# Moving the last sum of w2 behind the key-value masks, and the zero rows of the FFN block from GpSimd to VectorE

## The chip, the cores and the metric

The kernel runs on one core of one Trainium2 chip. The metric is the device time of one execution in microseconds, lower is better; medians of several executions are quoted. Each execution also has a *span*, the time from its first to its last recorded instruction. The device time is longer than the span, by something between 1.2 and 1.7 us in this case; I call the difference the *time outside the span*, and it will matter.

In lines of a profile PE is TensorE's matrix products and PEld its weight loads, DVE is VectorE, ACT ScalarE, POOL GpSimd and SP SyncE; L819 is line 819 of the kernel, and `<-` in brackets names what ended the idle time before.

## The reference, cut to what matters

```python
xn = layernorm(x)                                  # x: 2048 x 640, bf16
q, k, v = split(xn @ wqkv)                         # 32 heads of 20
pq, pk = phi(q), phi(k)
kv  = einsum("bhsd,bhse->bhde", pk, v)             # linear attention
s   = (pq @ kv) / (pq @ sum(pk)) @ wo
g   = silu(relu(xn @ w1) @ w2)                     # w1: 640 x 1728, w2: 1728 x 640
out = x + s * g
```

1728 is thirteen and a half blocks of 128, so the last block of the FFN's hidden rows is half used and its other rows must be zero. Those are the "zero rows".

## The kernel before: the parts concerned

The kernel computes the FFN product with a scheme of seven block products in place of eight. For that it needs four sums and differences of blocks of w2, made once by VectorE (`u_T(1)` to `u_T(4)`), and sums of blocks of the hidden layer (`u_S`). Close to the same place it forms the key-value matrix of all heads in one product, keeps the blocks on the diagonal by multiplying with a mask (`kv_group`), and multiplies them with wo (`W_block`).

```python
def kv_group(cs, b):                      # called for ps bank 5, then for ps bank 7
    ...                                   # 15 matmuls on PE into ps[b]
    tt(o_..., ps[b][...], mv6[...], ALU.mult, ...)      # the mask, on VectorE

def W_block(c, b):                        # banks b, b+1
    sc.group("PE", [... wo ...], R=[("wo", c), ("kv", c)], W=[("ps", b), ("ps", b + 1)])
    ...                                   # copy out (VectorE for c in 1, 4, else ScalarE)
    ...                                   # small DMAs on SP put the rows together

    u_T(2)
    divide(0)
    ...
    u_T(4)                                # the last sum of w2: 128 x 2240
    ...
    for n, fn in enumerate(us):           # us: the seven products of the first pair
        fn()
        if p == 0:
            if n == 0:
                kvs()                     # both kv_groups
            if n == 1:
                W_block(0, 4)
                W_block(1, 6)
```

A small scheduler gives every instruction its waits from what it reads and writes. Each engine works its list in order, so the place of `u_T(4)` in the text is its place in VectorE's queue. The constants, the zero rows among them, are made by GpSimd some way into the FFN's first layer:

```python
def build_consts():
    sc.op("POOL", lambda eng: eng.memset(hT[:, NF, :], 0.0), W=[("hz",)])   # 128 x 2048, bf16
    sc.op("POOL", lambda eng: eng.memset(sel[:, :], 1.0 / 32), W=[("sel",)])
    ...
```

Of the kernel before, what the change touches and what calls it, by code (L numbers as in the profile page):

```python
# [208 lines left out]
def bass_recurrent_scan__linear_attn_block__dense_activation_relu__prompt_kernel(  # L209
# [18 lines left out]
    NF = FF // P  # L228
# [36 lines left out]
    hT = regH[:, :].rearrange("p (f s) -> p f s", f=NK)  # L265
# [87 lines left out]
    sc = Sched(nc, NDS)  # L353
# [38 lines left out]
    def wk_load(k0, k1):  # L392
# [2 lines left out]
            W=[("wk", k) for k in range(k0, k1)])  # L395

    sc.op("DVE", lambda eng: eng.memset(zero[:, :], 0.0), W=[("zero",)])
    sc.op("ACT", lambda eng: eng.activation(out=msum[:, 3, 0:1], in_=zero[:, 0:1], func=ACTF.Copy),
          R=[("zero",)], W=[("msum", 3, 0)])
    sc.allow_unread.add(("msum", 3, 0))  # L400
# [29 lines left out]
    fill(32)  # L430

    def build_consts():
        sc.op("POOL", lambda eng: eng.memset(hT[:, NF, :], 0.0), W=[("hz",)])
        sc.op("POOL", lambda eng: eng.memset(sel[:, :], 1.0 / 32), W=[("sel",)])
        for u, base, mul in ((0, P // 2 - 1, -1), (1, -P // 2, 1)):
            sc.op("POOL", lambda eng, u=u, base=base, mul=mul: eng.affine_select(
                out=sel[:, u:u + 1], in_=sel[:, u:u + 1], compare_op=ALU.is_ge, fill=0.0, base=base, pattern=[[0, 1]],
                channel_multiplier=mul), R=[("sel",)], W=[("sel",)])
        sc.op("POOL", lambda eng: eng.memset(mh[:, :, :], 1.0), W=[("mh",)])
        sc.op("POOL", lambda eng: eng.affine_select(out=mh[:, :, :], in_=mh[:, :, :], compare_op=ALU.is_ge, fill=0.0,  # L440
                                                    base=0, pattern=[[P, C], [-DH, H]], channel_multiplier=1),
              R=[("mh",)], W=[("mh",)])
        sc.op("POOL", lambda eng: eng.affine_select(out=mh[:, :, :], in_=mh[:, :, :], compare_op=ALU.is_ge, fill=0.0,
                                                    base=DH - 1, pattern=[[-P, C], [DH, H]], channel_multiplier=-1),
              R=[("mh",)], W=[("mh",)])
        for lo, n, off in ((0, 6, 0), (6, 2, P - 2 * DH)):
            mt = mv6[:, lo:lo + n]
            key = ("mv6", lo)
            sc.op("POOL", lambda eng, mt=mt: eng.memset(mt, SC), W=[key])
            sc.op("POOL", lambda eng, mt=mt, n=n, off=off: eng.affine_select(  # L450
                out=mt, in_=mt, compare_op=ALU.is_ge, fill=0.0, base=-off, pattern=[[-DH, n]], channel_multiplier=1),
                R=[key], W=[key])
            sc.op("POOL", lambda eng, mt=mt, n=n, off=off: eng.affine_select(
                out=mt, in_=mt, compare_op=ALU.is_ge, fill=0.0, base=off + DH - 1, pattern=[[DH, n]], channel_multiplier=-1),
                R=[key], W=[key])
# [283 lines left out]
    def hz(keys):  # L739
        return sc._hazards([], keys)  # L740
# [62 lines left out]
    def load_recip(i):  # L803
        r = RS[i]
        keys = [("xnT", t) for t in range(12, T)] if r == 0 else [("zhi",), ("zlo",)] + ekeys + \
            [("gS", 1, q) for q in (1, 2, 4)]
        dma("SP", lambda eng: eng.dma_start(Rr[r], scr[:, schunk(i)].rearrange("(m p) s -> p m s", p=P)),
            R=[("scr", i)], W=[("Rr", r)], extra=hz(keys))
# [9 lines left out]
    def tt(out, in0, in1, op, R, W, extra=()):  # L818
        sc.op("DVE", lambda eng: eng.tensor_tensor(out=out, in0=in0, in1=in1, op=op), R=R, W=W, extra=extra)  # L819
# [322 lines left out]
    for c in range(VC):  # L1142
        r0 = VR * c if c < VC - 1 else D - P
        dma("SP", lambda eng, c=c, r0=r0: eng.dma_start(wo_sb[:, c, :], A_wo[r0:r0 + P, :]),
            W=[("wo", c)], extra=[last_norm[0]])
# [99 lines left out]
    def kv_group(cs, b):  # L1245
        fns = []
        for i, c in enumerate(cs):
            n0, n1 = VR * c, min(VR * c + VR, D)
            r0 = VR * c if c < VC - 1 else D - P
            for k in range(C):  # L1250
                fns.append(lambda eng, k=k, i=i, n0=n0, n1=n1, r0=r0: eng.matmul(
                    ps[b][:, VR * i:VR * i + n1 - n0], lhsT=wv_sb[:, k, r0:r0 + P], rhs=GT[:, k, n0:n1],
                    start=(k == 0), stop=(k == C - 1), skip_group_check=True))
        sc.group("PE", fns, R=[("wv",)] + gtk, W=[("ps", b)])
        for part in ([c for c in cs if c < VC - 1], [c for c in cs if c == VC - 1]):
            if not part:
                continue
            c0, nc_ = part[0], len(part)
            n0 = VR * c0
            nh = (min(n0 + VR, D) - n0) // DH  # L1260
            m0 = 0 if c0 < VC - 1 else 6
            st = D + VR
            q0 = VR * (c0 - cs[0])
            o_ = reg3[:, st * c0:st * (c0 + nc_)].rearrange("p (c x) -> p c x", x=st)[:, :, 0:nh * DH]
            tt(o_.rearrange("p c (h e) -> p c h e", e=DH),
               ps[b][:, q0:q0 + nc_ * nh * DH].rearrange("p (c h e) -> p c h e", c=nc_, e=DH),
               mv6[:, m0:m0 + nh].unsqueeze(1).unsqueeze(3).to_broadcast([P, nc_, nh, DH]), ALU.mult,
               [("ps", b), ("mv6", m0)], [("kv", c) for c in part], [lastG])
# [50 lines left out]
    def u_T(i):  # L1319
        b11, b12 = w2_sb[:, 0:KH, 0:HN], w2_sb[:, 0:KH, HN:D]  # L1320
        b21, b22 = w2_sb[:, KH:NK, 0:HN], w2_sb[:, KH:NK, HN:D]
        if i == 3:
            tt(uT[3], b22, b12, ALU.subtract, w2keys, [("uT", 3)], hz([("gT", 2)]))
        elif i == 2:
            tt(uT[2], uT[3], b11, ALU.add, w2keys + [("uT", 3)], [("uT", 2)], hz([("gT", 3)]))
        elif i == 4:
            tt(uT[4], b21, uT[2], ALU.subtract, w2keys + [("uT", 2)], [("uT", 4)], hz([("gT", 4)]))
        else:
            tt(uT[1], b12, b11, ALU.subtract, w2keys, [("uT", 1)], hz([("gT", 1)]))
# [174 lines left out]
    def flush():  # L1504
        while late:
            late.pop(0)()
# [40 lines left out]
    divide(0)  # L1547
    load_recip(1)
    load_recip(2)
    u_T(4)  # L1550

    def load_xre():
        for jx in range(4):
            dma("SP", lambda eng, jx=jx: eng.dma_start(
                xre[:, 4 * jx:4 * jx + 4, :], x2[512 * jx:512 * (jx + 1), :].rearrange("(t p) n -> p t n", p=P)),
                W=[("xre", jx)], extra=[lastG])

    def kvs():
        kv_group([0, 1, 2], 5)
        kv_group([3, 4, 5], 7)  # L1560


    for p in range(8):
        us = U_steps(p)
        os_ = O_steps(p - 1) if p else None
        at = 1
        for n, fn in enumerate(us):
            fn()
            if p == 0:
                if n == 0:  # L1570
                    kvs()
                if n == 1:
                    W_block(0, 4)
                    W_block(1, 6)
                if n == 2:
                    W_block(2, 4)
                    u_S(1, (1, 2))
                if n == 3:
                    W_block(3, 6)
                    W_block(4, 4)  # L1580
                    u_S(1, (3, 4))
                if n == 4:
                    W_block(5, 6)
                    load_xre()
                    late22.pop()()
                    u_S(2, (1, 2))
                    divide(1)
                    load_recip(3)
                continue
            if n == 0:  # L1590
                flush()
                if 1 < p < 7:
                    u_S(p + 1, (1, 2))
            if p > 1 and at <= n < at + 4:
                k = n - at
                for fn2 in os_[2 * k:2 * k + 2]:
                    fn2()
            if p == 1 and n == 1:
                divide(2, (0,))
            if p == 1 and n == 4:  # L1600
                s_tile(pairs[0][0], 0)
            if p == 1 and n == 5:
                s_tile(pairs[0][1], 2)
                o_S(1)
            if p == 7 and n == 5:
                flush()
                s_tile(pairs[7][0], 2)
            if n == 4:
                late22.pop()()
            if n == (5 if p == 2 else 2 if p == 3 else 1) and 1 < p < 7:  # L1610
                o_S(p)
            if p == 1 and n == 3:
                u_S(2, (3, 4))
            if n == at + 1:
                if p == 1:
                    o_T()
                elif p < 7:
                    u_S(p + 1, (3, 4))
                if p in (2, 4, 5):
                    divide(*{2: (2, (1,)), 4: (3, (0,)), 5: (3, (1,))}[p])  # L1620
# [34 lines left out]
```

## Time and profile before

| | |
|---|---|
| device time, median of three timed runs | 209.35 us (209.14 to 209.63) |
| device time of the run that was profiled | 210.28 us |
| span of the profiled run | 209.0 us |
| time outside the span, profiled run | 1.28 us |

The page's fourth part, the chain of work that ended last, by engine:

```profile
PE 86%; DVE 6%; DMA 5%; issue 1%; SPq 0%
```

It goes through a DMA and then VectorE. The timeline of VectorE shows where: the first sum of w2 starts when the last of w2 has landed (start, duration, what, idle before it and what ended that).

```profile
123.11 1.33 DVE L819 TENSOR_TENSOR reg<-reg 128x2240 f16<-128x2240 bf16 x1 [1.99 <-DMA reg<-in_B_w_dram]
```

From there to the masks VectorE has no idle.

### The profile page before, as it was taken

The page shows a single profiled execution, that of the slowest core. Times are in us where ns is not written, and L with a number is a line of the kernel's source. Part 1 is how long each engine was busy: PE and PEld are TensorE (multiplying, and loading weights), DVE is VectorE, ACT ScalarE, POOL GpSimd, SP SyncE. Part 2 cuts the span into 40 slices and gives each one's busy share as a digit, 9 for nine tenths or more (in the row PEclk, how much of TensorE's full clock was granted, in tenths as well). Part 3 has the DMA queues.
Part 4 walks back from the last instruction along what each step waited for, and adds up shares of the span by engine and source line. Part 5 has one row for each costly group of instructions (what it writes and reads, how often), then busy time and mean ns, then how long its engine had stood idle before and what let it go on. Part 6 is the DMA issues. An engine that isn't in the chain of part 4 may idle for free.

```text
span 209.0 us, 3733 instructions
## 1 busy us (share of the span) xinstructions
PE 205.1 (98%) x1401; PEld 127.0 (61%) x1401; DVE 165.0 (79%) x365; ACT 120.8 (58%) x243; POOL 21.3 (10%) x54
## 2 busy tenths in 40 slices
PE   8999999999999999999999999999999999999995
PEld 7755555545555444444456777677777777777773
DVE  3888757768999858686879759898888989897465
ACT  6497767787787987786563435362435254343531
POOL 1176015711210000000000000000000000000001
DMA  6998896130136000301224999246941010110103
GB/s 196 330 297 168 219 257 94 31 63 2 39 59 186 0 5 0 125 0 26 102 63 108 245 343 376 98 123 219 362 148 63 3 63 28 38 63 0 63 3 127
DMA packets 33063, 24.74 MB, mean 118 GB/s; under 512 B 12821, under 2 KB 33045, under 8 KB 33045
## 3 DMA queue, kind: packets, MB, share of 16 engines
q1 hardware_dynamic: 31813, 23.13, 39.2%
q10 hardware_dynamic: 1232, 1.37, 1.9%
q8 instruction: 11, 0.18, 0.4%
q14 instruction: 7, 0.06, 0.1%
HBM read 15.81 MB, written 5.24 MB: 101 GB/s over the span
## 4 chain that ended last, share of the span: by engine, by line
PE 86%; DVE 6%; DMA 5%; issue 1%; SPq 0%
PE psT L874 33%; PE psT L650 14%; PE psT L1029 11%; PE psT L551 11%; PE psT L601 10%; DMA reg<-in_B_w_dram 4%; DVE reg L819 2%; PE psT L1486 2%; DMA reg<-in_A_x_dram 1%; PE psT L668 1%; PE psT L1277 1%; DVE reg L1474 1%; DVE regE L819 1%; PE psT L525 1%; DVE pqT L812 1%
## 5 line engine op out<-in xcount | busy, mean ns | idle before, releaser
L874 PE MATMUL psT<-reg,regH 128*128 128x320 bf16 (+1 forms) x224 | 34.3, 299 | 0.0
L874 PE MATMUL psT<-reg 128*128 128x320 bf16 (+1 forms) x164 | 27.7, 299 | 0.0
L874 PEld LDWEIGHTS psT<-reg,regH 128*128 128x128 bf16 (+1 forms) x224 | 21.9, 98 | 8.5
L819 DVE TENSOR_TENSOR psT<-psT,reg 128x320 f32<-128x320 f32 (+1 forms) x33 | 16.4, 513 | 12.0 <-PE psT L874 8.8
L1311 ACT ACTIVATE wv_sb<-psT 128x320 bf16<-128x320 f32 x28 | 11.3, 436 | 25.2 <-PE psT L874 15.6
L601 PE MATMUL psT<-reg 128*128 128x512 bf16 x100 | 24.7, 379 | 0.0
L561 ACT ACTIVATE regE<-psT 128x640 bf16<-128x640 f32 x24 | 15.6, 701 | 8.1 <-PE psT L551 8.1
L874 PEld LDWEIGHTS psT<-reg 128*128 128x128 f16 (+1 forms) x164 | 16.0, 98 | 6.9 <-DVE regH L819 0.2
L881 ACT ACTIVATE psT<-psT 128x320 f32<-128x320 f32 x32 | 13.6, 426 | 11.2 <-PE psT L874 10.7
L881 ACT ACTIVATE reg<-psT 128x320 f32<-128x320 f32 (+1 forms) x24 | 10.4, 435 | 15.6 <-PE psT L874 13.6
L650 PE MATMUL psT<-reg 128*128 128x512 bf16 x75 | 18.5, 379 | 0.0
L654 ACT ACTIVATE regH<-psT 128x512 bf16<-128x512 f32 x28 | 16.5, 608 | 3.2 <-PE psT L650 3.2
L551 PE MATMUL psT<-reg 128*128 128x320 bf16 x120 | 18.3, 299 | 0.0
L461 DVE BATCH_NORM_STATS2 stats<-reg 128x6 f32<-128x320 bf16 x32 | 14.1, 475 | 4.7 <-DMA reg<-in_A_x_dram 4.7
L601 PEld LDWEIGHTS psT<-reg 128*128 128x128 bf16 x100 | 9.6, 98 | 11.0 <-issue 0.7
L551 PEld LDWEIGHTS psT<-reg 128*128 128x128 bf16 x120 | 11.7, 98 | 6.5
L1479 POOL TENSOR_TENSOR reg<-reg 128x224 bf16<-128x224 bf16 x1 | 0.6, 604 | 146.6 <-DVE reg L1474 146.6
L819 DVE TENSOR_TENSOR reg<-reg 128x1024 f16<-128x1024 bf16 (+6 forms) x17 | 13.6, 809 | 2.3 <-DMA reg<-in_B_w_dram 2.0
L650 PE MATMUL psT<-regX,reg 128*128 128x512 bf16 x65 | 14.8, 379 | 0.0
L874 PE MATMUL psT<-reg,pqT 128*128 128x320 bf16 (+1 forms) x72 | 14.7, 299 | 0.0
L1474 DVE TENSOR_TENSOR reg<-psT,wv_sb 128x640 bf16<-128x640 f32 (+2 forms) x16 | 11.7, 739 | 3.4 <-PE psT L874 1.8
L1029 PE MATMUL psT<-reg 128*128 128x512 bf16 x48 | 14.0, 379 | 0.0
(145 smaller groups left out, 354.1 us busy)
## 6 DMA issues: line engine op xcount, KB each, us to landing
reg<-in_B_w_dram SPq DMA_DIRECT2D x12, 320.0 KB, 6.0
scr<-rden SPq DMA_DIRECT2D x4, 640.0 KB, 8.8
reg<-in_A_x_dram SPq DMA_DIRECT2D x4, 640.0 KB, 6.5
out_dram<-reg SPq DMA_DIRECT2D x15, 160.0 KB, 1.9
reg<-in_A_x_dram SPq DMA_DIRECT2D x13, 160.0 KB, 5.0
regE<-scr SPq DMA_DIRECT2D x3, 640.0 KB, 8.1
reg<-in_A_wo_dram SPq DMA_DIRECT2D x6, 160.0 KB, 3.1
reg<-in_A_wqkv_dram SPq DMA_DIRECT2D x1, 800.0 KB, 5.3
```

The costliest lines, as they stand in the source:

```text
L461: sc.op("DVE", lambda eng: eng.bn_stats(stats[:, t, a, :], xv[:, HN * a:HN * (a + 1)]), R=[("xin", t % XR)], W=[("stats", t, a)])
L551: fns.append(lambda eng, a=a, k=k, lhs=lhs: eng.matmul(ps[b + a][:, 0:HN], lhsT=lhs, rhs=wk[:, k, HN * a:HN * (a + 1)], start=(k == 0), st ...
L561: sc.op("ACT", lambda eng: eng.activation(out=o_.rearrange("p (a n) -> p a n", a=2), in_=ps2(b, HN), func=func, scale=scale), R=[("ps", b) ...
L601: sc.group("PE", [(lambda eng, k=k: eng.matmul(ps[b], lhsT=wq[:, k, P * f:P * (f + 1)], rhs=xnT[:, j, k, :], start=(k == 0), stop=(k == C ...
L650: sc.group("PE", [(lambda eng, k=k: eng.matmul(ps[b], lhsT=w1_col(k, P * f, P), rhs=src[:, k, :], start=(k == 0), stop=(k == C - 1))) for ...
L654: return lambda: sc.op("ACT", lambda eng: eng.activation(out=hT[:, f, schunk(j)], in_=ps[b], func=ACTF.Relu), R=[("ps", b)], W=[("hT", j, f)])
L819: sc.op("DVE", lambda eng: eng.tensor_tensor(out=out, in0=in0, in1=in1, op=op), R=R, W=W, extra=extra)
L874: sc.group("PE", [(lambda eng, k=k, lhs=lhs, rhs=rhs: eng.matmul(ps[b][:, 0:HN], lhsT=lhs, rhs=rhs, start=(start and k == 0), stop=(k == n ...
L881: sc.op("ACT", lambda eng: eng.activation(out=dst, in_=ps[b][:, 0:HN], func=ACTF.Copy), R=[("ps", b)], W=[dkey], extra=extra)
L1029: sc.group("PE", [(lambda eng, k=k, lhs=lhs, rhs=rhs: eng.matmul(ps[b], lhsT=lhs, rhs=rhs, start=(start and k == 0), stop=(k == n - 1), sk ...
L1311: sc.op("ACT", lambda eng: eng.activation(out=g[:, HN * n:HN * (n + 1)], in_=ps[b][:, 0:HN], func=ACTF.Silu), R=[("ps", b)], W=[("g", sl, ...
L1474: sc.op("DVE", lambda eng: eng.tensor_tensor(out=tmpo[:, os_, lo:hi].rearrange(shp, a=na), in0=src, in1=g_of(t)[0][:, lo:hi].rearrange(shp ...
```

## The change

Its intent is to let the masks, for which TensorE waits, go ahead of a sum that is not needed until 5 us later, and to take a fill that collides with VectorE's work at 35 us out of the way.

```diff
     sc.op("DVE", lambda eng: eng.memset(zero[:, :], 0.0), W=[("zero",)])
+    sc.op("DVE", lambda eng: eng.memset(hT[:, NF, :], 0.0), W=[("hz",)])
 ...
     def build_consts():
-        sc.op("POOL", lambda eng: eng.memset(hT[:, NF, :], 0.0), W=[("hz",)])
 ...
     load_recip(2)
-    u_T(4)
 ...
                 if n == 0:
                     kvs()
+                    u_T(4)
```

## The prediction

> **What bounds the kernel now.** I read the page first, for the engine that is never short of work, then the waits of that engine, then the timeline around its only late wait, and last the first four microseconds and the place where the GpSimd fill runs.
>
> ```profile
> PE 205.1 (98%) x1401; PEld 127.0 (61%) x1401; DVE 165.0 (79%) x365; ACT 120.8 (58%) x243; POOL 21.3 (10%) x54
> ```
>
> TensorE is busy for 205.1 of 209.0 us, so a part of the change can only shorten the run where TensorE stands still, or at the two ends, where something else starts it or finishes after it. The waits of PE, of PE's weight loads after 100 us, and of GpSimd say where that is (columns: engine line waited for, us in total, times, longest):
>
> ```profile
> PE psT L426 <- PEq L1640: 0.8, 1, 0.8
> PE psT L1277 <- DVE reg L819: 0.4, 1, 0.4
> ...
> PEld psT L1277 <- DVE reg L819: 1.0, 2, 0.7
> ```
>
> After the start there is one wait in the whole run. Line 1277 is the product of the masked key-value blocks with wo; line 819 is the helper through which VectorE does its tensor-tensor sums, so its timeline is needed to see which of them it was. PE there (start us, duration, what):
>
> ```profile
> 130.07 1.60 PE L1251 MATMUL psT<-reg,wv_sb 128*128 128x120 bf16 x30
> 131.51 1.11 PE L874 MATMUL psT<-reg,regE 128*128 128x320 f16 x7
> ...
> 133.44 0.11 PEld L1277 LDWEIGHTS psT<-reg 128*128 128x128 bf16 x2 [0.31 <-DVE reg L819]
> 133.45 0.45 PE L1277 MATMUL psT<-reg 128*128 128x320 bf16 x2
> ...
> 133.73 1.11 PE L874 MATMUL psT<-regX,regE 128*128 128x320 f16 x7
> ```
>
> and VectorE in the same stretch:
>
> ```profile
> 129.74 1.55 DVE L812 TENSOR_TENSOR pqT<-pqT,reg 128x1024 bf16<-128x1024 bf16 x2
> 131.21 1.32 DVE L819 TENSOR_TENSOR reg<-reg,regX 128x2240 f16<-128x2240 bf16 x1
> 132.44 0.95 DVE L819 TENSOR_TENSOR reg<-psT,mv 128x360 bf16<-128x360 f32 x3
> 133.93 0.82 DVE L1282 CAST reg<-psT 120x640 bf16<-120x640 f32 x1 [0.54 <-PE psT L1277]
> 134.88 0.50 DVE L819 TENSOR_TENSOR psT<-psT,reg 128x320 f32<-128x320 f32 x1
> ```
>
> The 1.32 us instruction at 131.21 is the last sum of w2, the one that is moved; the three behind it are the masking. The key-value products (30 matmuls from 130.07) are finished at 131.66, but VectorE does the sum first, and PE waits twice: the first wo block for the first mask (0.41 us in PE's own record), the second, at 133.45, for the third mask, which reads the bank that this block overwrites.
>
> The fill of the zero rows, and the head:
>
> ```profile
> 35.34 1.80 POOL L433 MEMSET regH<- 128x2048 bf16 x1
> 35.43 1.94 DVE L489 TENSOR_SCALAR reg<-reg,mv,rsy 128x640 bf16<-128x640 bf16 x1 [0.99 <-POOL rsy L469]
> ...
> 0.86 0.06 DVE L397 MEMSET zero<- 128x1 bf16 x1 [0.86 <-PEq L1640]
> 3.36 0.49 DVE L461 BATCH_NORM_STATS2 stats<-reg 128x6 f32<-128x320 bf16 x1 [2.44 <-DMA reg<-in_A_x_dram]
> ```
>
> The VectorE normalisation that starts beside the GpSimd fill takes 1.94 us where the median of its 16 instances is 0.445. In the head VectorE has 2.44 us of nothing before the first tile of x lands.
>
> **What the Trainium skill says.** "Perfetto Trace Analysis", section "Identifying the Most-Contended Engine", warns that busy share overstates TensorE because matmuls are pipelined; the trace agrees: the 7 matmuls at 131.51 span 1.11 us on record, but 14 in a row at 138.62 reach the next group 1.90 us later, 0.136 us each. I therefore count PE by starts, not by idle. "SBUF — State Buffer", section "Who interferes with whom", says that a GpSimd instruction and a VectorE instruction in a two-port mode (tensor_scalar can be one) exclude each other for the whole instruction; 1.94 us against 0.445 beside a 1.80 us fill agrees, as the part of the fill still to run when it started, 37.14 - 35.43 = 1.71, plus part of its own 0.445 is about what it took. It also says that a VectorE instruction with at most one SBUF input outside those modes does not contend. "VectorE: DVE Perf Modes", section "Zero memsets can be issued as uint32 (trn2)", gives one cycle per element for a memset of any type, and its specifications 0.96 GHz: 2048 elements are an estimated 2.13 us. No large VectorE memset is in this trace to check it.
>
> **The change part by part.**
>
> *The sum moved behind the masks.* Without any wait PE would have gone on from 131.51 as follows: 7 matmuls x 0.136 = 0.95, so 132.46 for the first wo block; 4 wo matmuls x 0.136 = 0.54, so 133.00 for the next group. It began at 133.73. The loss is 0.73 us, more than the 0.41 shown as idle: about 0.16 is the overlap of the last matmul's tail and the rest is the second wait.
>
> After the change the first mask waits for VectorE's divide, which leaves the engine at about 131.21 (its successor starts then now), and for the first half of the key-value products (15 x 0.048 after 130.07 plus a tail of 0.16, so 130.95): it starts near 131.21 and takes 0.53, done at 131.75, ahead of 132.46. The second and third need the second half, 131.66, plus a hand-over of 0.05: 131.72, then 0.4 and 0.2, done near 132.25, ahead of 132.73 when the second wo block is due. Both waits go. VectorE then does the sum from about 132.1 to 133.4; the copy of the second wo block (product ready near 133.16) starts at 133.4 against 133.93 now; the add after it needs PE's group from 133.00, over at 134.11, so it starts near 134.2 against 134.88. VectorE thus follows PE's shift within 0.05. The sum itself is needed by the product that PE starts at 138.62 now and about 137.9 then; it is there at 133.4. Gain on PE: 0.73 us. The work is the same on every engine.
>
> *The fill.* GpSimd loses 1.80 us at 35.34; VectorE gains about 2.13 in the head and gets back 1.94 - 0.445 = 1.49 at 35.43. VectorE in the head: 0.92 + 2.13 = 3.05 (3.21 if some 0.15 of fixed time comes with it), before 3.36. Nothing on the path. At 35 us PE does not wait, as its list shows, so the 1.49 us shorten VectorE's queue and nothing else: 0.0. I expect GpSimd's next useful rsqrt, queued behind its constants until 40.06 now, to come about 1.7 us earlier, also hidden.
>
> Sum: 0.73 + 0.0, so the span goes from 209.0 to about 208.3 and the median from 209.35 to 208.6. The ending after PE's last product keeps its length.
>
> **Rivals.**
>
> *A DMA wait takes the place of the removed one.* The first attention tile behind the wo blocks (weight load at 144.19 now) needs a sum of the reassembled weights that VectorE starts at 143.33, held by the last of ten small copies. SP issues those ten in one row from 134.24 to 141.9, 0.74 us each (median), so the row moves only with its first issue, which follows ScalarE's copy of the first wo block. That copy runs at 133.51 now; ScalarE is busy with another copy from 132.66, whose successor can start some 0.34 later, so it moves to about 133.00, by 0.51 and not by 0.73. The sum would then be ready at 143.33 - 0.51 + 0.53 + 0.05 = 143.40, and PE asks at 144.19 - 0.73 = 143.46. It fits by 0.06. If the row moves less, say 0.3, PE waits 0.15 and the gain is 0.58; if it does not move, the gain is 0.36. For it: SP's row is tight. Against: everything in front of it moves. I take off 0.05 for it: 208.65.
>
> *The fill overruns the head.* Should VectorE's memset end after 3.36, every us of overrun is lost at once, for the chain that ended last begins with that DMA and that statistics instruction. At two cycles an element it would end at 5.2 and cost 1.8 us, giving 210.5. Against: the page's one cycle. A faster mode only adds slack. A memset that locked GpSimd out would delay the identity (done at 1.51, first used at 4.54) by at most 2.2 us, harmless.
>
> *The faster middle shows.* If VectorE's 1.49 us shifted PE there the gain would be up to 2.2 us, 207.1. Against: PE runs gapless from 9.7 us to 132.6.
>
> **Range and chances.** Predicted 208.65 us. The three runs before spread over 0.5 us, so a median is uncertain by some 0.2; the mechanism by 0.1 to 0.4 down and a little up. A range of 208.2 to 209.2 should hold it 8 times in 10. Faster by over 2% would need below 205.2, slower above 213.5: 0.005 each, and 0.99 for within 2%.
>
> **What would show it.** Right: no wait of line 1277 for line 819 on PE or PEld; the group after the second wo block starts near 133.0, and from there all of PE runs 0.7 earlier; the sum is seen after the masks. A VectorE memset of about 2.1 us starts near 0.92 and the statistics still start at 3.36; the normalisation near 35.4 falls to about 0.45. Wrong: a new wait of line 1486 for VectorE or a DMA near 143.5 (first rival), a statistics start after 3.4 (second), a PE that is ahead already at 100 us (third), or a PE saving that VectorE's queue between 134 and 142 does not follow.

## The result, and the profile after

| | before | after |
|---|---|---|
| device time, median | 209.40 us (209.14 to 209.63, 4 runs) | 209.85 us (209.70 to 210.26, 4 runs) |
| ratio | | 1.0025, interval 1.0007 to 1.0043 |
| span of the profiled run | 209.0 us | 208.3 us |
| time outside the span, profiled run | 1.28 us | 1.53 us |

The predicted 208.65 us was missed by 1.2 us, and the direction is wrong, though both effects are far inside 2%.

What makes this instructive is that the trace of the changed kernel looks exactly as foretold. Its page, first part and chain by engine:

```profile
PE 204.0 (98%) x1401; PEld 126.3 (61%) x1401; DVE 164.8 (79%) x366; ACT 120.8 (58%) x243; POOL 19.4 (9%) x53
...
PE 94%; DMA 2%; DVE 1%; issue 0%; SPq 0%
```

TensorE's waits (line waited for: us in total, times, longest) and its timeline around the wo blocks:

```profile
PE psT L551 <- DMA reg<-in_A_wqkv_dram: 0.9, 1, 0.9
PE psT L427 <- PEq L1640: 0.8, 1, 0.8
```

```profile
131.51 1.11 PE L874 MATMUL psT<-reg,regE 128*128 128x320 f16 x7
132.46 0.71 PE L1277 MATMUL psT<-reg 128*128 128x320 bf16 x4
133.00 1.11 PE L874 MATMUL psT<-regX,regE 128*128 128x320 f16 x7
```

The wo blocks start at 132.46 and the next group at 133.00, to the hundredth as worked out, and the span is 0.7 us shorter. The hundredth is chance: both traces happen to reach the key-value products at 130.07, while those of e0 to e3 below reach them at 129.86 to 130.25. What recurs is the distance from there to the first wo block, 2.39 us in every trace here without a wait for the masks. VectorE in the same kernel:

```profile
122.32 1.33 DVE L819 TENSOR_TENSOR reg<-reg 128x2240 f16<-128x2240 bf16 x1 [1.19 <-DMA reg<-in_B_w_dram]
...
131.06 1.16 DVE L819 TENSOR_TENSOR reg<-psT,mv 128x360 bf16<-128x360 f32 x3 [0.56 <-PE psT L1251]
132.13 1.32 DVE L819 TENSOR_TENSOR reg<-reg,regX 128x2240 f16<-128x2240 bf16 x1
```

The masks now come ahead of the sum. But the first line is the catch: w2 landed 0.79 us earlier than in the trace of before, and nothing in the change touches w2. VectorE even stands idle for 0.56 us ahead of the masks. With w2 this early the old order should have had the masks ready in time as well (argued here; e0 and e2 below show it). So the comparison of these two traces mixes the change with a chance difference, and says nothing yet about what the change is worth. And the time went up while the span went down, so something outside the span grew.

The fill, in the head and at 35 us:

```profile
1.10 0.91 DVE L398 MEMSET regH<- 128x1024 uint32 x1 [0.18 <-issue]
...
3.07 0.49 DVE L461 BATCH_NORM_STATS2 stats<-reg 128x6 f32<-128x320 bf16 x1 [1.06 <-DMA reg<-in_A_x_dram]
...
35.40 0.45 DVE L489 TENSOR_SCALAR reg<-reg,mv,rsy 128x640 bf16<-128x640 bf16 x1 [0.99 <-POOL sel L434]
```

The fill ends at 2.01, well before x lands at 3.07, and the normalisation at 35 us is back from 1.94 to 0.45 us.

### The profile page after: what moved, and what is told of

The parts are those of the page before. It is cut to its first block, busy times and chain, and to the rows that moved or that the text cites. A ratio compares the mean times of both kernels' runs of the same rounds, so it can differ in the third digit from the quotient of the medians. Undisturbed runs are those within 1.5% of the kernel's fastest.

```text
span 208.3 us, 3731 instructions
## 1 busy us (share of the span) xinstructions
PE 204.0 (98%) x1401; PEld 126.3 (61%) x1401; DVE 164.8 (79%) x366; ACT 120.8 (58%) x243; POOL 19.4 (9%) x53
## 4 chain that ended last, share of the span: by engine, by line
PE 94%; DMA 2%; DVE 1%; issue 0%; SPq 0%
PE psT L874 39%; PE psT L650 15%; PE psT L1029 11%; PE psT L601 10%; PE psT L551 10%; DMA reg<-in_A_wqkv_dram 2%; PE psT L1538 2%; PE psT L1486 2%; PE psT L668 1%; DVE reg L1474 1%; PE psT L1277 1%; PE psT L1251 1%; PE psT L748 1%; PE psT L778 1%; DVE reg L1479 0%
```

## The experiments

Fifteen runs. Theory A: the wait that the change removes exists only when w2 lands late, which is rare. Rival B: it is in every run of before, and something outside the span gives its 0.7 us back. Rival C: the 0.25% is scatter between runs. For the loss outside the span, at first: the fill itself, or a count of instructions.

### The kernel before against itself (e0)

No edit.

> The kernel before, unchanged, against itself. Theory A (the wait of the wo block depends on when w2 lands): its spans differ from run to run, most near 208.3 with no wait of line 1277, a few near 209.0 with the 0.73 us loss; ratio 1.000. Theory B (the wait is in every run of before and the gain of 0.7 us was given back outside the span): spans all near 209.0, time minus span near 1.3. Rival C (the 0.25% is a difference between runs taken at different moments): ratio may be off 1.000 by 0.2% although nothing was changed.

Measured: median 209.72 us against 209.28, ratio 1.0014, interval 0.9996 to 1.0032. The spans of its six runs go from 207.8 to 208.7 us, those of the eleven runs of before beside it from 207.6 to 208.9; none is at 209.0. The time outside the span is 1.21 to 1.31 us in all 17. Its waits and VectorE:

```profile
PE psT L426 <- PEq L1640: 0.8, 1, 0.8
PE psT L1251 <- DMA wv_sb<-in_A_wqkv_dram: 0.6, 1, 0.6
```

```profile
121.52 1.33 DVE L819 TENSOR_TENSOR reg<-reg 128x2240 f16<-128x2240 bf16 x1 [0.98 <-DMA reg<-in_B_w_dram]
...
131.24 1.16 DVE L819 TENSOR_TENSOR reg<-psT,mv 128x360 bf16<-128x360 f32 x3 [0.30 <-PE psT L1251]
```

The same kernel, the old order, and no wait for the masks: w2 landed 1.6 us earlier than in the first trace. In place of it TensorE waited 0.6 us for another load, a part of wqkv. Rival B is out. The run also shows what scatter is here: 0.14% between a kernel and itself.

### Each part alone, and both again (e1, e2, e3)

e1, the sum alone:

```diff
-    u_T(4)
 ...
                     kvs()
+                    u_T(4)
```

> Only the sum of w2 moved behind the masks. Theory A: span 208.3, ratio 0.997 to 1.000 by how often before had the wait. Theory B: span 208.3, ratio 0.9965 if the reordering gains and the fill is what gives it back.

e2, the fill alone:

```diff
     sc.op("DVE", lambda eng: eng.memset(zero[:, :], 0.0), W=[("zero",)])
+    sc.op("DVE", lambda eng: eng.memset(hT[:, NF, :], 0.0), W=[("hz",)])
 ...
-        sc.op("POOL", lambda eng: eng.memset(hT[:, NF, :], 0.0), W=[("hz",)])
```

> Only the fill moved to VectorE in the head. If the fill is what costs: ratio 1.002 to 1.004, time minus span 1.5 instead of 1.3 or a span that is longer by 0.3 to 0.7. If it is harmless: ratio 1.000 and the same spans as before.

e3, the changed kernel as it is:

> The changed kernel again. If the result on record holds: ratio 1.0025 with an interval that excludes 1, spans 208.2 to 208.7. Rival C: ratio within 0.1% of 1.000.

| run | median, us | ratio, interval | spans, mean (range) | outside the span, mean (range) |
|---|---|---|---|---|
| before | 209.28 | | 208.10 (207.6 to 208.9) | 1.27 (1.21 to 1.30) |
| e1, sum | 209.26 | 1.0001 (0.9977 to 1.0025) | 208.12 (207.7 to 209.0) | 1.27 (1.24 to 1.31) |
| e2, fill | 209.86 | 1.0025 (1.0008 to 1.0042) | 208.35 (208.0 to 208.8) | 1.52 (1.47 to 1.59) |
| e3, both | 209.57 | 1.0021 (0.9999 to 1.0044) | 208.27 (207.7 to 208.9) | 1.53 (1.48 to 1.56) |

The sum is worth nothing that can be seen, and the fill carries the loss. The last column is far sharper than the times: 0.25 us more on average with the fill on VectorE, and the ranges don't touch. So rival C, scatter alone, does not explain the loss, though e3's own interval includes 1 and the 0.14% of e0 is more than half of it. e2 has the old order; its VectorE shows it, and its list of PE waits has no line of the wo blocks:

```profile
122.27 1.32 DVE L819 TENSOR_TENSOR reg<-reg 128x2240 f16<-128x2240 bf16 x1 [1.12 <-DMA reg<-in_B_w_dram]
...
131.60 0.95 DVE L819 TENSOR_TENSOR reg<-psT,mv 128x360 bf16<-128x360 f32 x3
```

Landed at 122.27, masks from 131.60, and that is just early enough.

### A VectorE that is always late (e4, e5)

To see the worth of the order apart from luck, one of the sums is done twice (with the same result), which delays VectorE by 1.33 us in every run. e4 is the old order, e5 the new one.

```diff
     u_T(2)
+    sc.allow_unread.add(("uT", 2))
+    u_T(2)
```

> The kernel before with one sum of w2 done twice, so that VectorE always comes about 1.33 us later to the masks, whenever w2 lands. If the order of the last sum and the masks costs PE time only when VectorE is late: PE waits for the masks by about 1.2 us (0.73 of the trace of before, plus 1.33, minus the 0.8 by which w2 usually lands earlier than in that trace); span about 209.3 in nearly every run. If the order never matters: span 208.1.

> The same doubled sum with the last sum behind the masks. If the reordering is worth what the prediction said whenever VectorE is late: PE waits by 0.1 us at most, span 208.1 to 208.2, so about 1.1 us less than with the old order. If it is worth nothing: the same span as the old order with the doubled sum.

e4: 210.35 us, ratio 1.0031 (1.0010 to 1.0053), spans 208.6 to 209.5, mean 209.08. e5: 209.40 us, ratio 0.9983 (0.9962 to 1.0005), spans 207.6 to 208.4, mean 208.03. Of e4, the wait of PE for the masks, and VectorE's last sum and masks; then the same part of VectorE in e5, whose list of PE waits has no such line:

```profile
PE psT L1277 <- DVE reg L819: 0.9, 1, 0.9
...
131.49 1.32 DVE L819 TENSOR_TENSOR reg<-reg,regX 128x2240 f16<-128x2240 bf16 x1
132.72 0.95 DVE L819 TENSOR_TENSOR reg<-psT,mv 128x360 bf16<-128x360 f32 x3
```

```profile
131.46 0.95 DVE L819 TENSOR_TENSOR reg<-psT,mv 128x360 bf16<-128x360 f32 x3
132.32 1.32 DVE L819 TENSOR_TENSOR reg<-reg,regX 128x2240 f16<-128x2240 bf16 x1
```

1.05 us of mean span between the two orders, as expected to 0.05. In e4 the second wo block starts at 133.73 in place of 132.53 (2.66 us after the key-value products, as in the runs without a wait), a loss of 1.20. The mechanism of the prediction is right; what was wrong is the belief that it is at work in an ordinary run.

How ordinary? The distance from the start of the first sum of w2 to the first key-value matmul tells how early VectorE is. In the trace that I predicted from it is 6.96 us. In the 13 other traces taken by then (after, and e0 to e11) it is 7.70 to 8.73. At 7.82 with the old order (e2) there was no wait, and by the 0.73 of the prediction none is left from about 7.69 (an estimate: 6.96 + 0.73). The first trace is the only one of 14 below that. Of the three taken later, e12 is at 8.72, and e13 and e14 are at 7.65 and 7.64, so the old order would have cost them some 0.05 us.

A long span alone is no sign of this wait. The traced run of e12 has the new order and yet a span of 209.1 us; in it TensorE waited 0.9 us for a part of wqkv:

```profile
PE psT L1254 <- DMA wv_sb<-in_A_wqkv_dram: 0.9, 1, 0.9
```

So the two of the eleven runs of before beside e4 with spans of 209.0 and 209.2 us can't be counted for either side; they have no trace.

### Whose count of instructions? (e6, e7)

The "closing hand-shake" or "release" of the texts below is the row of steps shown in the table of semaphore steps under e12 to e14; the late one is its third from the end.

e6 is the changed kernel with the one-element memset of `zero` on GpSimd; e7 is e1 with one more one-element memset on VectorE.

```diff
-    sc.op("DVE", lambda eng: eng.memset(zero[:, :], 0.0), W=[("zero",)])
+    sc.op("POOL", lambda eng: eng.memset(zero[:, :], 0.0), W=[("zero",)])
```

> The changed kernel with the one-element zero memset given to GpSimd, so that VectorE has as many instructions as before and still does the fill. If it is VectorE's count of instructions that makes the time outside the span 1.53 instead of 1.27: back to 1.27, and the late step of the closing hand-shake 0.04 instead of 0.28. If it is the fill itself: stays at 1.53.

```diff
+    pad = nc.alloc_sbuf_tensor("pad", [P, 1], bf)
+    sc.op("DVE", lambda eng: eng.memset(pad[:, :], 0.0), W=[("pad",)])
```

> Only the sum moved, the fill left on GpSimd, and one extra one-element memset on VectorE in the head. If VectorE's count of instructions is the cause: time minus span 1.53. If the fill is: 1.27.

Outside the span: e6 1.27 to 1.30 us, e7 1.26 to 1.32 us (times 209.53, ratio 0.9999, and 209.36, ratio 0.9989). e6 did what the theory of VectorE's count asked, e7 did not: VectorE has an instruction more there than in e1 and nothing happened. (e4, with one more than the kernel before, was at 1.22 to 1.26 too.) e6 has the fill on VectorE and is at 1.28, so it is not the fill either. What e6 restored is the number of GpSimd's instructions. My theory fell, and a better one stood in the same numbers.

### GpSimd's count, without the fill and with it (e8 to e11)

e8: e1 with the fill on GpSimd still, but in GpSimd's own idle head.

```diff
     sc.op("POOL", lambda eng: eng.memset(mhalf[:, :], -0.5), W=[("mhalf",)])
+    sc.op("POOL", lambda eng: eng.memset(hT[:, NF, :], 0.0), W=[("hz",)])
 ...
-        sc.op("POOL", lambda eng: eng.memset(hT[:, NF, :], 0.0), W=[("hz",)])
```

> The sum moved, and the fill kept on GpSimd but put into GpSimd's own idle head; no engine has another count of instructions than before. If the 0.26 us outside the span come with GpSimd's count: time minus span 1.27, the normalisation near 35.4 us back to about 0.45 us as in the changed kernel, span near 208.1, ratio 0.998 to 1.000. If a fill in the head costs wherever it is done: 1.53.

e9: the changed kernel with an idle memset added to GpSimd.

```diff
+    pad = nc.alloc_sbuf_tensor("pad", [P, 1], bf)
+    sc.op("POOL", lambda eng: eng.memset(pad[:, :], 0.0), W=[("pad",)])
```

> The changed kernel with one extra one-element memset on GpSimd. GpSimd's count (62 records as in the kernel before): time minus span 1.27, third step of the release 0.04. The fill on VectorE: 1.53 and 0.28.

e10: e1 with a memset of two elements taken from GpSimd to VectorE; the fill stays on GpSimd. e11: the changed kernel with the same edit.

```diff
+    sc.op("DVE", lambda eng: eng.memset(sel[:, :], 1.0 / 32), W=[("sel",)])
 ...
-        sc.op("POOL", lambda eng: eng.memset(sel[:, :], 1.0 / 32), W=[("sel",)])
```

> Only the sum moved, fill left on GpSimd in its old place, but a memset of two elements taken from GpSimd to VectorE. GpSimd's count (61): time minus span 1.53. The fill: 1.27.

> The changed kernel with that two-element memset also taken from GpSimd (60 records). If fewer GpSimd instructions simply mean a later close: 1.53 or more. If it is a matter of one particular length: may be back at 1.27. If only the fill matters: 1.53.

The texts above count all records of GpSimd in the trace, 62 in the kernel before; the page's first part, which leaves out waits and the like, shows 54 of them. (PE x1390 in the lines below: some matmul records are missing from those traces.)

| run | fill on | GpSimd records | outside the span, us | median, us | ratio, interval |
|---|---|---|---|---|---|
| e8 | GpSimd, head | 62 | 1.25 (1.22 to 1.30) | 209.33 | 0.9994 (0.9978 to 1.0010) |
| e9 | VectorE | 62 | 1.28 (1.23 to 1.31) | 209.39 | 1.0002 (0.9988 to 1.0016) |
| e10 | GpSimd, old place | 61 | 1.52 (1.48 to 1.54) | 209.87 | 1.0018 (1.0000 to 1.0036) |
| e11 | VectorE | 60 | 1.66 (1.58 to 1.70) | 209.68 | 1.0012 (0.9995 to 1.0029) |

e9 and e10 cross the two suspects, and GpSimd's count wins both times: the fill on VectorE with 62 records costs nothing, and 61 records without any moved fill cost the 0.25 us. The records of VectorE (454 to 456) and of ScalarE (275 or 276) do not sort the runs: each of these numbers occurs with and without the delay. TensorE's and SyncE's are the same in all. The first part of the pages, e9 and then e10, shows the place of the fill in the busy time of POOL (19.4 without, 21.7 with it) and the count behind it:

```profile
PE 203.9 (98%) x1390; PEld 127.0 (61%) x1401; DVE 164.7 (79%) x366; ACT 120.7 (58%) x243; POOL 19.4 (9%) x54
```

```profile
PE 204.0 (98%) x1390; PEld 127.3 (61%) x1401; DVE 165.1 (79%) x366; ACT 120.7 (58%) x243; POOL 21.7 (10%) x53
```

e8 answers what the fill's move itself can give. GpSimd's fill sits in its head, and the collision at 35 us is gone as well:

```profile
1.50 1.80 POOL L424 MEMSET regH<- 128x2048 bf16 x1
...
35.59 0.45 DVE L489 TENSOR_SCALAR reg<-reg,mv,rsy 128x640 bf16<-128x640 bf16 x1 [1.00 <-POOL sel L434]
```

That is 1.49 us of VectorE's time less than in the trace of before, and a mean span of 208.07 against 208.06 of before beside it: nothing, as TensorE doesn't wait there.

### Other lengths of GpSimd's program (e12, e13, e14)

e1 with one, two and four idle one-element memsets on GpSimd.

```diff
+    pad = nc.alloc_sbuf_tensor("pad", [P, k], bf)               # k = 1, 2, 4
+    for i in range(k):
+        sc.op("POOL", lambda eng, i=i: eng.memset(pad[:, i:i + 1], 0.0), W=[("pad", i)])
```

> Only the sum moved, plus one one-element memset on GpSimd (63 records). If a shorter GpSimd program closes later in steps (60: 1.66, 61: 1.52, 62: 1.25): time minus span 1.25 or less. If 62 is only one good length among bad ones: 1.5 or more.

> The same with two such memsets (64 records). Steps: 1.25 or less. A good length by chance: anything from 1.25 to 1.7.

> The same with four such memsets (66 records). Steps: 1.25 or less. A good length by chance: anything from 1.25 to 1.7.

| GpSimd records | 60 | 61 | 62 | 63 | 64 | 66 |
|---|---|---|---|---|---|---|
| outside the span, mean, us | 1.66 | 1.52 | 1.25 to 1.28 | 1.43 | 1.55 | 1.30 |
| its range | 1.58 to 1.70 | 1.48 to 1.54 | 1.22 to 1.31 | 1.38, 1.47 | 1.46, 1.64 | 1.26, 1.33 |
| run | e11 | e10 | e8, e9 | e12 | e13 | e14 |

e12 to e14 are two runs each (medians 210.03, 209.60 and 209.24 us, ratios 1.0034, 1.0014, 0.9997, intervals about 0.5% wide or more to each side, so only the column outside the span is read). Shorter is not the point: 63 and 64 are bad too, and 66 is good again, as far as two runs each can say. The kernel before happens to have a good length.

One semaphore (number 2 of the trace) is still counted up after the work is done, and it shows where some of the delay is. These are the steps between its last nine increments, all after the last instruction that the span counts, in ns:

```
before (62)  35  65  43  23  99   39  34  47
e9     (62)  34  38  45  23  98   39  34  46
after  (61)  35  38  44  23  99  276  35  46
e10    (61)  34  38  43  24  99  275  34  47
e12    (63)  34 216  45  23  98   39  34  46
e11    (60)  34  38  44  23  99   38  35  46
e13    (64)  34  44  44  23  99   38  34  47
```

With 61 one step takes 0.275 in place of 0.039 us: the 0.24 us of the loss. With 63 another step is late. With 60 and 64 none is, though those runs were late by 0.4 and 0.2 us; their delay must lie where this semaphore does not show it. Why these lengths are late stays open. Fetching of instructions would fit a dependence on length, and the traces record some of it, as DMA transfers of the kind "instruction": from 206 us on, only e13 and e14 have one, of 8 KB. In e14, which is not late, it starts 0.49 us before the end of the span; in e13, which is late, 1.39 us after it. With 60, 61 and 63 no such transfer is on record there, so this is a lead and not the cause.

No version beats the kernel before. e8 is the clean form of the change's intent, at 0.9994, which is the same time.

## Why the prediction was wrong, point by point

- **The loss of 0.73 us in the trace, and that the reordering removes it.** Right as mechanism. With a VectorE made late, the old order loses 1.20 us by TensorE's starts and the new one wins 1.05 us of mean span over it. The times worked out for after were met: 132.46 and 133.00 for TensorE, 133.4 for the copy (133.37), 134.2 for the add (134.16).
- **"so the span goes from 209.0 to about 208.3 and the median from 209.35 to 208.6".** This is the step that failed. It took a loss found in one execution off the median of others. That the profiled run of before was 0.93 us over the median was a hint that the two don't go together; e0 and e2 show that at usual landings of w2 an execution holds none of this loss. The gain for an ordinary run was mis-sized: 0.73 predicted, nothing measured (e1: 1.0001). The mark-down of "0.05" was for a different doubt.
- **The fill: 0.0 in the path.** Right inside the span. The term of its duration was too long: 2.13 us estimated, 0.91 on record, where the compiled program fills 1024 words of four bytes instead of 2048 of two, the very form that the section cited there describes. The collision at 35 us was read rightly: as "SBUF — State Buffer", section "Who interferes with whom", has it of GpSimd and a VectorE instruction in a two-port mode (that this one was in such a mode is not shown), the normalisation took 1.94 us beside GpSimd's fill and 0.45 without it. It is worth nothing, as predicted (e8). GpSimd's next rsqrt came 2.0 us earlier (38.06 against 40.06), where 1.7 had been expected.
- **"The ending after PE's last product keeps its length."** This is the second step that failed. The prediction summed what lies inside the span only. Taking one instruction from GpSimd lengthened the time outside it by 0.25 us. That term was absent. It is half of the measured 0.25% (0.52 us); the other half is within what the kernel showed against itself in e0 (0.14%, 0.3 us).
- **The first rival, the DMA wait ahead of the attention tile.** It didn't come: VectorE waited 0.41 us for the small copies, TensorE not at all. The sum that holds the tile started at 142.81, where 143.33 - 0.51 gives 142.82. (One sum of this rival is off: with a row that does not move, its own terms give 143.91 against 143.46, a wait of 0.45 and a gain of 0.28, not 0.36.)
- **Range.** 208.2 to 209.2 allowed for 0.2 us of scatter about a typical run. That the 0.73 us itself might be one run's luck was not in it. "Within 2%" held.

## What to carry to other kernels

Before taking a wait out of a trace, compare the time of the profiled run with the median; if it lies far off, that is a warning, though no proof. A wait that hangs on the landing of a DMA may be that run's own, and further traces of the same kernel show whether it is. To value an order of work apart from luck, force the lateness that it is meant for and compare both orders. And look at time minus span: here a column that stays within 0.1 us for one kernel (1.21 to 1.31 in e0 and the runs of before beside it) found what the times, which range over 1.2 us there (208.90 to 210.13), could only hint at.

## What the Trainium skill lacked or had wrong

- "VectorE: DVE Perf Modes", section "Zero memsets can be issued as uint32 (trn2)", says that it pays to do so; it doesn't say that it can happen unasked. The source fills bf16, and the trace has 128x1024 uint32 at 0.91 us. At the page's cycle per element and 0.96 GHz that would be an estimated 1.07 us, so the record is also 0.16 shorter than that.
- None of the pages that I consulted has it that the length of GpSimd's program changes the time outside the span: means of 1.25 to 1.30 us with 62 or 66 records, 1.43 to 1.66 with 60, 61, 63 or 64. "Runtime: NRT & Kernel Launch", section "Instruction fetch mechanics", has it that instructions are streamed in blocks and that this is mostly hidden; whether these delays are that, no run here shows.
